# An attention and expert kernel: engine overlap in the scheduler's cost model, and one more head pair transposed by DMA

## The chip, the cores and the metric

The kernel runs on one NeuronCore of a Trainium2 chip. The metric is the device time of one execution in microseconds (us); a kernel's figure is the median of its runs. The clock of TensorE that the hardware granted is known for every run, and no run of this study was in a slow state, so all runs are compared with each other. Engines are named as in the profile: PE is TensorE, PEld its weight load, DVE is VectorE, ACT ScalarE, POOL GpSimd, SP SyncE. GpSimd and SyncE issue DMAs, each into a queue of its own (the rows POOLq and SPq of the page).

## The reference

```python
def _attn_ref(q, k, v):                      # 4 batches x 8 heads x 768 x 64
    k_sum = k.reshape(B, H, nb, 32, D).max(axis=3)      # a summary of each 32 keys
    v_sum = v.reshape(B, H, nb, 32, D).mean(axis=3)
    scores_l = scale * q @ k^T, kept where |pos_q - pos_k| < 16
    scores_s = scale * q @ k_sum^T + log(32)
    a = softmax over both together
    return a @ concat(v, v_sum)

def _moe_ref(x, w_gate, w1, w2):             # x: 3072 x 512, 8 experts, 1024 hidden
    P = exp(x @ w_gate - max)
    8 times: normalize P by rows, by columns, times N / E
    out = sum over e of P[:, e] * (relu(x @ w1[e]) @ w2[e])
```
(Abridged to pseudocode; the attention's output, reshaped, is x.)

## The kernel before

The 32 heads are handled as 16 pairs, two heads of 64 columns side by side. The experts' matmuls are woven between the steps of attention, so that TensorE always has something to do. The weaving is made while the program is built: every step is a unit with an engine, a cost in us, and the units it depends on, and a list scheduler picks the order in which each engine issues its units.

```python
class Plan:
    HOP = 0.15
    ...                                            # (cut)
    def order(self):
        ...
                for e, cost in u.eng.items():      # a unit may have a choice of engines
                    t = max([t0, free.get(e, 0.0)]
                            + [d.end + d.lag + (self.HOP if d.on != e else 0.0) for d in u.deps])
                    best.setdefault(e, []).append((t, u, cost))
        ...
            u.start, u.end, u.on = t, end, e
            free[e] = end                          # the engine is free when its unit ends
```

What comes out is a fixed order for each engine. In these traces an engine that comes to an instruction which must wait stands there (TensorE for 4.28 us in the kernel after). `lag` is the planned time between the end of issuing a DMA and its landing.

The parts of attention that matter here, for a "whole" pair i (4 to 15, made by `pair_whole`; the constant `WHOLE` is another matter). The keys and queries arrive as rows and must be transposed; before pair `BY_DMA` TensorE does it, from there on a DMA transpose from SyncE. The values of one 128-row chunk need 16 rows from each neighbouring chunk; four small copies, SBUF to SBUF by DMA, put them into `V_e`. I call them the **bordering copies**.

```python
    BY_DMA = 12
    X_BY_DMA = 12
    WHOLE = 10
    ...
    def tr(i, z): ...            # 6 TensorE transposes into PSUM, copied out by ScalarE or VectorE
    def tr_dma(i, z):
        st = at.pop(("st", i, z))
        dst = (kT[i % NB][:], qT[i % NB][:, W:W + S])[z]
        nc.sync.dma_start_transpose(out=dst.rearrange("c (g t) -> c g t", g=G),
                                    in_=st[:].rearrange("p g j d -> p (g j d)"))
    ...
    def near_values(i):
        sv, ve = v_x[i % NQ], V_e[i % NE]
        eng = nc.sync if i < BY_DMA else nc.gpsimd
        for j in range(2):
            c0, q0 = VD * j, 64 + 32 * j
            eng.dma_start(out=ve[q0 + W:q0 + 2 * W, 1:G, c0:c0 + VD], in_=sv[128 - W:128, j, 0:G - 1, :])
            eng.dma_start(out=ve[q0:q0 + W, 0:G - 1, c0:c0 + VD], in_=sv[0:W, j, 1:G, :])
    ...
    def values(i, h):            # unit A: exp(scores) times values
        ...                      # 6 matmuls  av <- vx, em   (the chunk itself)
        ...                      # 3 matmuls  av <- Ve, Ee   (borders and summaries: needs V_e)
    ...
        # in pair_start
            if i >= BY_DMA:
                for z in range(2):
                    U["tr", i, z] = add("SP", 1.4, lambda z=z: tr_dma(i, z), ...)
                    U["kT", i, z] = add("DMA", 1.7, None, [U["tr", i, z]], prio, lag=2.0)
    ...
        # in pair_whole
            U["near", i] = add("SP" if i < BY_DMA else "POOL", 2.4 if i < BY_DMA else 3.0,
                               lambda: near_values(i),
                               [U["v", i], U.get(("A", i - NE, 1)), U["vc", i % NE]], prio,
                               lag=5.0 if i < BY_DMA else 3.5)
    ...
            for h in range(2):
                U["A", i, h] = add("PE", 0.4, lambda h=h: values(i, h),
                                   [U["mk", i, h], U["ed", i], U["sx", i, h], U["Vs", i], U["near", i]], ...)
```

So `BY_DMA` sets two things: who transposes a pair's k and q, and whose queue carries its bordering copies. The loads of k, q and v for these pairs are issued from GpSimd. Line numbers of the kernel after are one higher than those of the kernel before (L441 there is L442 here).

Of the kernel before, what the change touches and what calls it, by code (L numbers as in the profile page):

```python
# [33 lines left out]
class Plan:  # L34

    HOP = 0.15

    def __init__(self, slots, idle=None):
        self.units, self.slots = [], slots
# [18 lines left out]
    def order(self):  # L58
        free, ring, turn = {}, {t: [None] * n for t, n in self.slots.items()}, {t: 0 for t in self.slots}
        left, n_left, after = [], {}, {}  # L60
        for u in self.units:
            n_left[u] = len(set(u.deps))
            for d in set(u.deps):
                after.setdefault(d, []).append(u)
            if not u.deps:
                left.append(u)
        done = []

        def ready(u):
            t = 0.0  # L70
            for i, b in enumerate(u.opens):
                old = ring[b.tag][(turn[b.tag] + i) % self.slots[b.tag]]
                if old is not None:
                    if any(x.start is None for x in old.users):
                        return None
                    t = max([t] + [x.end + (self.HOP if x.on not in u.eng else 0.0) for x in old.users])
            return t

        while left:
            best = {}  # L80
            for u in left:
                t0 = ready(u)
                if t0 is None:
                    continue
                for e, cost in u.eng.items():
# [3 lines that stand above are left out]
            picks = []  # L89
            for e, c in best.items():  # L90
                t_min = min(t for t, _, _ in c)
                t, u, cost = min((x for x in c if x[0] <= t_min + 0.02), key=lambda x: x[1].prio)
                picks.append((t, t + cost, e, u, cost))
            t, end, e, u, cost = min(picks, key=lambda x: x[:2])
            if self.idle is not None:
                us, fn, until = self.idle
                if until.start is not None:
                    self.idle = None
                while self.idle is not None and t > free.get("PE", t) + us:
                    x = Unit("PE", us, fn, [], 0.0, [Buffer("m")], 0.0)  # L100
                    x.opens[0].users.append(x)
                    t0 = ready(x)
                    if t0 is None or t0 + us > t:
                        break
                    x.start = max(t0, free["PE"])
                    x.end = free["PE"] = x.start + us
                    if x.end > t:
                        break
                    x.on = "PE"
                    ring["m"][turn["m"] % self.slots["m"]] = x.opens[0]  # L110
                    turn["m"] += 1
                    done.append(x)
            u.start, u.end, u.on = t, end, e
            free[e] = end
            for b in u.opens:
                ring[b.tag][turn[b.tag] % self.slots[b.tag]] = b
                turn[b.tag] += 1
            left.remove(u)
            done.append(u)
            for x in after.get(u, ()):  # L120
                n_left[x] -= 1
                if not n_left[x]:
                    left.append(x)
        assert len([u for u in self.units if u.start is None]) == 0
        return done
# [3 lines left out]
def kernel(  # L129
# [12 lines left out]
    B, H, S, D = q.shape  # L142
# [14 lines left out]
    HG = G // 2  # L157
    VD = D + 1
    NEH = 3
    BY_DMA = 12  # L160
    X_BY_DMA = 12
    WHOLE = 10
    FILL = {"v0": 1, "S0": 1, "s0": 2, "s1": 1, "s2": 1}

    const = ctx.enter_context(tc.tile_pool(name="const", bufs=1))
# [60 lines left out]
    with tc.manual_schedule():  # L226
# [155 lines left out]
        def scores(i):  # L382
            sg = at["sg", i, 0] = banks2("sg")
            dst = [[sg[:, j, :] for j in range(2)], None]
            if i >= WHOLE:
                dst[1] = at["sg", i, 1] = [bank("a", "sg1") for _ in range(2)]
            score_mms(i, dst, range(G if i >= WHOLE else HG))

        def scores_1(i):
            sg = at["sg", i, 1] = banks2("sg")  # L390
# [553 lines left out]
        def pair_whole(i, prio):  # L944
            U["near", i] = add("SP" if i < BY_DMA else "POOL", 2.4 if i < BY_DMA else 3.0, lambda: near_values(i),
                               [U["v", i], U.get(("A", i - NE, 1)), U["vc", i % NE]], prio, lag=5.0 if i < BY_DMA else 3.5)
            x1 = []
            deps = [U["kT", i, 0], U["kT", i, 1], U.get(("ed", i - 2))]
            bufs = [Buffer("s")] + (2 * [None] if i < WHOLE else [Buffer("a"), Buffer("a")])
            U["S", i, 0] = U["S", i, 1] = add("PE", 0.4 if i < WHOLE else 0.6, lambda: scores(i), deps, prio,  # L950
                                              opens=[x for x in bufs if x is not None])
            U["X", i, 0] = add("ACT", 0.97, lambda: score_exp(i, 0), [U["S", i, 0]], prio, uses=bufs[:1])
            if i < WHOLE:
                buf = Buffer("s")
                U["S", i, 1] = add("PE", 0.4, lambda: scores_1(i), deps, prio, opens=[buf])
                U["X", i, 1] = add("ACT", 0.97, lambda: score_exp(i, 1), [U["S", i, 1], U["X", i, 0]], prio,
                                   uses=[buf])
            else:
                x1 = [add("ACT", 0.53, lambda j=j: score_exp(i, 1, j), [U["S", i, 0], U["X", i, 0]], prio,
                          uses=bufs[1 + j:2 + j]) for j in range(2)]  # L960
                U["X", i, 1] = x1[1]
            for h in range(2):
                U["mk", i, h] = add("DVE", 0.56, lambda h=h: masks(i, h),
                                    [U["X", i, h], *x1[:h], U.get(("A", i - 2, 1))], prio)
            U["ed", i] = add("DVE", 0.78, lambda: edges(i),
                             [U["X", i, 0], U["X", i, 1], U["mk", i, 1], U.get(("A", i - NE, 1)), U["ec", i % NE]], prio)
            buf = Buffer("a")
            U["ss", i, 0] = U["ss", i, 1] = add("PE", 0.22, lambda: summaries_2(i),
                                                [U["km", i], U["kT", i, 1], U.get(("A", i - NE, 1))], prio, opens=[buf])
            for h in range(2):  # L970
                U["sx", i, h] = add("ACT", 0.46, lambda h=h: summary_exp(i, h), [U["ss", i, h]], prio, uses=[buf])
            for h in range(2):
                buf = Buffer("a")
                U["A", i, h] = add("PE", 0.4, lambda h=h: values(i, h),
                                   [U["mk", i, h], U["ed", i], U["sx", i, h], U["Vs", i], U["near", i]],
                                   prio, opens=[buf])
                U["no", i, h] = add("DVE", 0.75, lambda h=h: normalize(i, h),
                                    [U["A", i, h], U.get(("x", i - 2))], prio, uses=[buf])
            if i >= X_BY_DMA and i % PB < PB - 1:
                U["xt", i] = add("SP", 1.5, lambda: x_dma(i), [U["no", i, 0], U["no", i, 1]], prio)  # L980
                U["x", i] = add("DMA", 1.7, None, [U["xt", i]], prio, lag=2.0)
                return
            buf = Buffer("a")
            U["xt", i] = add("PE", 0.35, lambda: to_xT(i), [U["no", i, 0], U["no", i, 1]], prio, opens=[buf])
            U["x", i] = add({"ACT": 0.8, "DVE": 0.55}, 0, lambda: x_out(U["x", i].on, i), [U["xt", i]], prio,
                            uses=[buf])
# [109 lines left out]
        def transposed():  # L1096
# [1 line left out]
            r = (NP - 1) % NB  # L1098
            nc.gpsimd.tensor_copy(out=warm[:, 0:1], in_=kT[r][0:32, 0:1])
            nc.gpsimd.tensor_copy(out=warm[:, 1:2], in_=qT[r][0:32, W:W + 1])  # L1100
            if X_BY_DMA < NP:
                nc.gpsimd.tensor_copy(out=warm[:, 4:5], in_=xT[0:32, PB - 2, (B - 1) * S:(B - 1) * S + 1])
            ve = V_e[(NP - 1) % NE]
            for j in range(2):
# [1 line left out]
                                      in_=ve[64 + 32 * j:96 + 32 * j, G - 2, VD * j:VD * j + 1])  # L1106

        last[0] = add("POOL", 0.3, transposed, [last[0], U["near", NP - 1]] + [U["kT", NP - 1, z] for z in range(2)]
                      + [U["x", i] for i in range(X_BY_DMA, NP - 1)])
        load("w1n", lambda: load_w1(1), 0.85, 5.0)  # L1110
        load("w2n", lambda: load_w2(1), 0.85, 5.0)
        U["w1", 1], U["w2", 1] = U["w1n"], U["w2n"]
        U["post"] = add("SP", 0.0, pools, [U["lo", b] for b in range(B)] + [last[0]])
        prev = [U["post"]]
        for n in range(8):
            rows = add("DVE", 1.65, sink_rows, prev, 0)
            buf = Buffer("Q")
            cols = add("PE", 0.1, sink_cols, [rows], 0, opens=[buf], lag=0.1)
            prev = [add("DVE", 0.6, sink_apply, [cols], 0, uses=[buf])]
# [201 lines left out]
```

## Time and profile before

| | before |
|---|---|
| time, median of the first 3 runs | 666.17 us (666.14 to 666.85) |
| span of the profiled run, granted clock | 664.1 us, 0.999 |
| TensorE busy | 99% |
| VectorE, ScalarE, GpSimd busy | 83%, 62%, 30% |
| DMA queue of SyncE (hardware) | 9.58 MB, 5.9% of 16 engines' span |
| pair 11's bordering copies: issued, last landed | 75.81 to 77.72 us from SyncE, 84.70 us |
| pair 11's first border matmul | 92.64 us |

The prediction shows the lines on which the bound rests. What it did not look at are the last two rows of the table: when pair 11's copies land and when TensorE wants them. Times of issue come from the timelines of SyncE and TensorE, times of landing, here and below, from the updates of the DMAs' semaphores in the packed trace; a pair is told apart by counting the groups of four copies and the groups of border matmuls. In the kernel before there are 7.9 us between the two.

### The profile page before, as it was taken

The numbers are of one execution on the slowest core, as the hardware profiler recorded it, in microseconds if no ns is written. First come the engines' busy times: TensorE is split into PE (matmuls) and PEld (weight loads), VectorE is DVE, ScalarE is ACT, GpSimd is POOL, SyncE is SP. The second block draws the span as 40 slices with busy tenths as digits, with TensorE's granted clock in tenths as the row PEclk, the third lists the DMA queues.
The fourth block names the chain that finished last, engine by engine and source line by source line (L and its number), as shares of the span: only waits on it lengthen the run. The fifth ranks groups of instructions, "written<-read, shape, count | busy, mean of one in ns | idle before, by whom it ended". The sixth has DMA issues, their size and how long they took to land.

```text
span 664.1 us, 13257 instructions
## 1 busy us (share of the span) xinstructions
PE 656.6 (99%) x5131; PEld 435.9 (66%) x5132; DVE 550.1 (83%) x1036; ACT 410.9 (62%) x769; POOL 199.0 (30%) x257
## 2 busy tenths in 40 slices
PE   8999999999999999999999999999999999999997
PEld 4666666545766666666666666666666666666666
DVE  7899897799988887887779877988778877988776
ACT  6677676556885566556665665555655656556652
POOL 8899522100132222212322222223122213222123
PEclk9999999999999999999999999999999999999999
DMA  9999932700953747373754665373838465335656
GB/s 167 181 145 145 143 70 43 128 1 2 157 96 65 126 75 118 64 128 65 110 97 71 121 91 101 64 127 65 127 64 135 73 96 96 64 64 112 157 134 202
DMA packets 112558, 67.89 MB, mean 102 GB/s; under 512 B 77936, under 2 KB 90480, under 8 KB 112496
## 3 DMA queue, kind: packets, MB, share of 16 engines
q0 software_dynamic: 94816, 57.46, 64.9%
q1 hardware_dynamic: 17152, 9.58, 5.9%
q8 instruction: 40, 0.66, 0.4%
q14 instruction: 22, 0.18, 0.1%
q10 hardware_dynamic: 528, 0.02, 0.0%
HBM read 52.45 MB, written 6.29 MB: 88 GB/s over the span
## 4 chain that ended last, share of the span: by engine, by line
PE 96%; DVE 3%; DMA 1%; issue 0%; ACT 0%; POOLq 0%; DVEq 0%
PE yps L815 22%; PE pA L764 22%; PE pY L815 17%; PE pQ L764 11%; PE hps L211 6%; PE yps L216 6%; PE pR L764 5%; PE sg L347 1%; DMA qst<-in_q_dram 1%; PE av L512 1%; PE vs L357 1%; PE tkq L303 1%; PE av L435 1%; DVE xs L543 1%; PE ss L461 1%; PE av L441 1%
## 5 line engine op out<-in xcount | busy, mean ns | idle before, releaser
L815 PEld LDWEIGHTS <-h 128*128 128x128 f16 x2352 | 230.1, 98 | 88.5 <-issue 1.0
L843 POOL DMA_DIRECT2D out_acc<-y x120 | 101.7, 891 | 372.1 <-ACT y L839 110.3
L839 ACT ACTIVATE y<-pY,P_sb 128x256 f32<-128x256 f32 x168 | 79.8, 477 | 123.3 <-PE pY L815 121.6
L830 DVE SCALAR_TENSOR_TENSOR out_acc<-yps,P_sb,out_acc 128x512 f32<-128x512 f32 x128 | 95.1, 744 | 29.0 <-PE yps L815 29.0
L798 DVE TENSOR_TENSOR h<-h 128x1024 f16<-128x1024 f16 x168 | 109.3, 683 | 1.4
L815 PE MATMUL pY<-w,h 128*128 128x256 f16 x672 | 100.0, 273 | 0.6 <-ACT y L839 0.6
L815 PE MATMUL yps<-w2sum,h 128*128 128x256 f16 x672 | 98.4, 273 | 0.0
L764 PE MATMUL pA<-xT,w 128*128 128x512 f16 x336 | 98.3, 379 | 0.0
L815 PE MATMUL yps<-w,h 128*128 128x256 f16 x672 | 93.3, 273 | 0.0
L830 DVE SCALAR_TENSOR_TENSOR out_acc<-pY,P_sb,out_acc 128x512 f32<-128x512 f32 x84 | 62.8, 748 | 29.1 <-PE pY L815 27.4
L764 PEld LDWEIGHTS <-w 128*128 128x128 f16 x672 | 65.8, 98 | 31.6 <-issue 0.2
L764 PEld LDWEIGHTS <-w1sum 128*128 128x128 f16 x504 | 49.3, 98 | 45.0
L786 DVE CUSTOM_DVE_ANT_0 h<-pQ,snap 128x512 f16<-128x512 f32 x84 | 57.6, 685 | 7.0 <-ACT snap L207 4.3
L786 DVE CUSTOM_DVE_ANT_0 h<-pA,snap 128x512 f16<-128x512 f32 x84 | 57.3, 682 | 4.8 <-PE pA L764 4.8
L202 ACT ACTIVATE h<-pA 128x512 f16<-128x512 f32 x84 | 50.6, 603 | 12.6 <-PE pA L764 12.4
L202 ACT ACTIVATE h<-pR 128x512 f16<-128x512 f32 x84 | 50.1, 596 | 8.0 <-PE pR L764 7.7
L207 ACT COPY pR<-pA 128x512 f32<-128x512 f32 x83 | 47.5, 572 | 7.7 <-PE pA L764 6.9
L815 PE MATMUL pY<-w2sum,h 128*128 128x256 f16 x336 | 50.4, 273 | 0.0
L764 PE MATMUL pA<-xsum,w 128*128 128x512 f16 x168 | 50.0, 379 | 0.0
L764 PE MATMUL pR<-xT,w 128*128 128x512 f16 x168 | 50.0, 379 | 0.0
L764 PE MATMUL pQ<-xsum,w1sum 128*128 128x512 f16 x168 | 50.0, 379 | 0.0
L764 PE MATMUL pA<-xsum,w1sum 128*128 128x512 f16 x168 | 50.0, 379 | 0.0
(150 smaller groups left out, 854.3 us busy)
## 6 DMA issues: line engine op xcount, KB each, us to landing
out_acc<-y POOLq DMA_DIRECT2D x120, 256.0 KB, 3.4
w<-in_moe_w_dram POOLq DMA_DIRECT2D x14, 1024.0 KB, 10.7
out_dram<-out_acc SPq DMA_DIRECT2D x24, 256.0 KB, 2.4
qst<-in_q_dram POOLq DMA_DIRECT2D x32, 96.0 KB, 5.3
vx<-in_v_dram POOLq DMA_DIRECT2D x15, 192.0 KB, 6.2
kst<-in_k_dram POOLq DMA_DIRECT2D x24, 96.0 KB, 5.6
w<-in_moe_w_dram POOLq DMA_DIRECT2D x4, 256.0 KB, 7.6
w<-in_moe_w_dram POOLq DMA_DIRECT2D x2, 512.0 KB, 7.7
```

What stands on the lines that cost most here:

```text
L202: nc.scalar.activation(out=out, in_=in_, func=AF.Relu, bias=0.0, scale=1.0)
L207: (nc.scalar.copy if eng == "ACT" else nc.vector.tensor_copy)(out=out, in_=in_)
L211: nc.tensor.matmul(hp[:, 0:n], lhsT=w1s[e][:, dk, f * 128:(f + 1) * 128], rhs=xT[:, dk, t0:t0 + n], start=(dk == 0), stop=(dk == KD - 1))
L216: nc.tensor.matmul(yp[:, d], lhsT=h[:, f, c * 128:(c + 1) * 128], rhs=w2s[e][:, f, d], start=(f == 0), stop=(f == KF - 1))
L303: nc.tensor.transpose(t[:, g * 128:(g + 1) * 128], st[:, g, :, :].rearrange("p j d -> p (j d)"), ident)
L764: nc.tensor.matmul(dst[:], lhsT=lhsT, rhs=rhs, start=first and k == 0, stop=k == HK - 1, skip_group_check=True)
L786: nc.vector._custom_dve(dve_ops.TENSOR_ADD_SAT, out=ring(e, p, q)[:, q % 2, blk, :], in0=at[src, e, p, q][:], in1=at.pop(("snap", n, e, p, ...
L798: nc.vector.tensor_tensor(out=h[:, :, out_, :], in0=h[:, :, a, :], in1=h[:, :, b, :], op=op)
L815: nc.tensor.matmul(dst[:, d], lhsT=lhsT, rhs=rhs, start=f == 0 and n in (1, 5, 2), stop=f == HF - 1, skip_group_check=True)
L830: nc.vector.scalar_tensor_tensor(out=o, in0=y, scalar=scalar, in1=o, op0=ALU.mult, op1=ALU.add)
L839: nc.scalar.activation(out=at[key][:, d], in_=src, func=AF.Copy, bias=0.0, scale=P_sb[:, t, e:e + 1])
L843: nc.gpsimd.dma_start(out=o, in_=at.pop(("y", e, p, c, key))[:], accum_op=ALU.add)
```

## The change

Two intents. The scheduler takes an engine as busy to the end of each unit, though VectorE and ScalarE start the next instruction a little before the last one has ended (0.08 and 0.09 us before, by the medians in the prediction); the change gives back 0.07 and 0.09 us for each unit and corrects one figure (sink rows, 1.65 to 1.5 us). And one more pair is transposed by DMA, which takes 12 transposes off TensorE.

```diff
+    OVERLAP = {"DVE": 0.07, "ACT": 0.09}
...
-            free[e] = end
+            free[e] = end - self.OVERLAP.get(e, 0.0)
...
-    BY_DMA = 12
-    X_BY_DMA = 12
-    WHOLE = 10
+    BY_DMA = 11
+    X_BY_DMA = {12, 13, 14}
+    WHOLE = {10, 11, 12, 13, 14, 15}
...
-            rows = add("DVE", 1.65, sink_rows, prev, 0)
+            rows = add("DVE", 1.5, sink_rows, prev, 0)
```

(Cut: the places that test `i in WHOLE` and `i in X_BY_DMA` in place of `>=`; the sets hold the same pairs as before.) What the diff doesn't say in words: with `BY_DMA = 11`, pair 11's bordering copies go from SyncE's queue to GpSimd's.

The text on record follows, with marks where passages are cut: statements of how the hardware behaves that no trace of this case shows. No term of its sum is cut: that is 0.67 us for the transposes and 0.22 us for fewer breaks between kinds, together 0.89 us, off 666.17, which gives 665.3 us. Its estimate of the time that the columns of all matmuls need is cut. The trace of the kernel before gives one in its place: the medians of 56 ns for 128 columns and 216 ns for 512 make 0.417 ns a column, and at that, each column counted once, an estimated 638.3 of the 664.1 us are columns. Three statements that stay, with their figures from the same trace: a matmul of 256 columns has a bar of 273 ns in the median and the next starts 109 ns after it; none of SyncE's 69 DMAs lands before an earlier one of SyncE; the DMA share between 40 and 80 us is 2.29.

> **What bounds the kernel now.** I read the page first: the table of busy time, the forty slices, then the chain that ended last.
>
> ```profile
> span 664.1 us, 13257 instructions
> ...
> PE 656.6 (99%) x5131; PEld 435.9 (66%) x5132; DVE 550.1 (83%) x1036; ACT 410.9 (62%) x769; POOL 199.0 (30%) x257
> ...
> PE   8999999999999999999999999999999999999997
> ...
> PEclk9999999999999999999999999999999999999999
> ...
> PE 96%; DVE 3%; DMA 1%; issue 0%; ACT 0%; POOLq 0%; DVEq 0%
> ```
>
> TensorE is busy in every slice but the first and the last, at the full clock, and 96% of the chain that ended last is TensorE work. VectorE, the next, has 17% of the span free. A change that only moves work between VectorE and ScalarE can therefore gain only where TensorE really waits for one of them.
>
> "Busy" is not enough to say so, because each matmul's bar overlaps the next one's. So I took the start of every matmul in the trace and the distance to the next start. Matmuls of 512 columns start 216 ns apart in the median, those of 256 columns 109 ns, those of 128 columns 56 ns. From 24 us on, three places alone show a wait beyond what a change from one group of matmuls to the next normally costs: 0.21 us before the logits at 65.9 us, 0.30 us (0.17 + 0.12) between 644.6 and 645.4 us, and 0.73 us at 657.5 us. In all 1.24 us in 640. The last of them is visible in the timeline of the tail:
>
> ```profile
> 657.21 0.60 PE L815 MATMUL pY<-w2sum,h 128*128 128x256 f16 x4
> 657.85 0.47 ACT L839 ACTIVATE y<-pY,P_sb 128x256 f32<-128x256 f32 x1 [2.09 <-PE pY L815]
> 658.37 0.60 PE L815 MATMUL pY<-w,h 128*128 128x256 f16 x4 [0.56 <-ACT y L839]
> ```
>
> A group adds into the bank that ScalarE is still reading; TensorE cannot go round it.
>
> [...]
>
> [...]VectorE's h sums last 682 ns in the median, yet the next instruction starts a median 602 ns after the start; ScalarE's copies into pR last 570 ns with 483 ns to the next start. It is seen in pairs in the timeline too:
>
> ```profile
> 647.52 0.83 ACT L839 ACTIVATE y<-pY,P_sb 128x256 f32<-128x256 f32 x2
> ...
> 651.10 1.46 DVE L830 SCALAR_TENSOR_TENSOR out_acc<-yps,P_sb,out_acc 128x512 f32<-128x512 f32 x2
> ```
>
> Two y of 0.47 us each fit in 0.83 us. So the new constants, 0.07 us for VectorE and 0.09 us for ScalarE, bring the scheduler's picture nearer the chip. Nothing runs faster for it: the constants only change the order in which instructions are issued, and which of two engines takes a copy.
>
> **The change part by part.**
>
> 1. Overlap and the sink figure (1.65 to 1.5 us). No instruction is added or removed. The built programs agree on TensorE in their first 655 rows (327 matmuls, up to 24.3 us in the trace of before) and in the last 49; between them the order differs. Copies shift to VectorE: snapshots from pA 29 to 40, from pQ 14 to 23, first scalings 6 to 10, while hidden relus go 17 to 10 the other way. That is 24 more and 7 fewer of these four kinds on VectorE. At some 0.6 us (from start to start) about 10 us of work moves to an engine with 114 us free. Cost on the path: none of itself.
>
> 2. Pair 11's q and k by DMA. This removes 12 TensorE transposes, 6 for k and 6 for q:
>
> ```profile
> 80.69 0.51 PE L303 MATMUL tkq<-ident,kst 128*128 128x128 bf16 x6
> 81.03 1.03 PE L216 MATMUL yps<-w,h 128*128 128x512 f16 x4
> ...
> 82.55 0.50 PE L303 MATMUL tkq<-ident,qst 128*128 128x128 bf16 x6
> 82.88 1.46 PE L211 MATMUL hps<-xT,w 128*128 128x384 f16 x8
> ```
>
> Measured from start to next start, not by the second column: 81.03 - 80.69 = 0.34 us and 82.88 - 82.55 = 0.33 us. Since TensorE has no free time there, **0.67 us** comes off the end. Two VectorE copies of 0.56 us out of PSUM go too, beside the path.
>
> What is added is two DMA transposes on the queue that issues from SyncE. [...]The trace has eight like them, and the row of the values that border on a chunk, which move from SyncE's queue to GpSimd's for this pair:
>
> ```profile
> Ve<-vx SPq DMA_DIRECT2D x32, 10.2 KB, 5.1
> ...
> Ve<-vx POOLq DMA_DIRECT2D x16, 10.2 KB, 1.9
> kT<-kst SPq DMA_TRANSPOSE x4, 5.5
> qT<-qst SPq DMA_TRANSPOSE x4, 4.9
> ```
>
> In before, pair 11's k and q have been requested by 58 us and its scores run at 84.28 us. A transpose issued near 66 us, where pair 12's now stands (66.23 us), would land near 72. The bordering values cost GpSimd four issues of 0.52 us right after its last value load (76.62 us) and should land near 82, about when SyncE's (75.81 us plus four issues and 5.1 us) did. So nothing of this lands on the path.
>
> 3. The new order as TensorE sees it. I priced each matmul of both built programs, from 24.3 us on, with the median start-to-next-start that the same kind with the same successor has in before (7 changes of kind in the new order have no equal there and got their kind's median). The new order comes out 0.89 us shorter: the 0.67 us above, and 0.22 us from fewer breaks between kinds. That is an estimate for an order without waits.
>
> Sum: 0.89 us off 666.17 gives 665.3. Of the 1.24 us of waits some may go, but the one of 0.73 us stands in the 49 last rows that do not change.
>
> **The rivals.** (a) New waits on TensorE. The old, pessimistic constants left slack: instructions came ready earlier than planned. With truer constants TensorE is asked for results closer to when they are there. For it: hundreds of dependent steps between 24 and 160 us. Against it: 0.07 and 0.09 us are still below the 0.08 to 0.09 us that I read. Expert matmuls fill that stage, so a late result holds TensorE for tenths of a us. I allow 0 to 1.5 us; then 665.3 to 666.8. (b) The waits at 65.9 and 645 us vanish and the logits come early, as the order suggests (the last logits stand 28 matmuls earlier, 12 of them the transposes): up to 0.5 us more gained, 664.8. (c) The transposes of pair 11 or the bordering values behind them come late, because SyncE's queue is in order and DMA is loaded to over twice its engines' time between 40 and 80 us. Pair 11 would be late by a few us, and filler would run instead only if the fixed order has it. It would cost 1 to 4 us, 666 to 669. The 12 us computed above speak against it. (d) VectorE becomes the bound among the experts: no, 10 us more of 550 leave it under 86%.
>
> **Range and chances.** Centre 665.3 us, from the sum with (a) and (b) about cancelling. Low 664.3: the sum with (b) and half a us of run-to-run spread (the three runs of before span 0.7 us). High 666.5: most of (a), no net gain. Two per cent is 13.3 us; ten times the removed waits would not make it, and only a broken order would cost it. Faster 0.01, same 0.98, slower 0.01.
>
> **What would show it right or wrong.** Right: 84 transposes into tkq from the later pairs instead of 96, TensorE's busy time about 0.7 to 0.9 us lower, its slices all 9 from the second to the last but one, the wait of about 0.7 us for y still there at the end, pair 11's kT landing 5 to 6 us after issue with no TensorE wait before its scores, VectorE some us busier and ScalarE less. Wrong: TensorE idle or stretched starts between 24 and 160 us that sum to over 1 us (rival a or c; the waits name which), or a gain over 1.5 us, which would mean that waits were hidden in the starts that I took as normal changes between groups.

## The result, and the profile after

The kernel after takes **675.4 us** in the median (674.15 to 676.8, 4 runs); the kernel before, with one more run beside them, 666.27 us (666.14 to 666.85, 4 runs). The ratio is **1.0134**, with a 95% interval of 1.0115 to 1.0153. A ratio here is the mean time of one kernel's fast runs over that of the other's in the same rounds, so it is not quite the ratio of the medians. At a threshold of 2% the verdict is still "same", yet the loss of 9 us lies far outside the spread. It is some ten times the predicted gain, with the other sign.

The page of the kernel after, the lines that answer to the prediction's first fence:

```profile
span 673.5 us, 13253 instructions
...
PE 661.0 (98%) x5119; PEld 436.9 (65%) x5120; DVE 563.0 (84%) x1051; ACT 401.6 (60%) x752; POOL 201.5 (30%) x261
...
PE   9999979999999999999999999999999999999997
...
PEclk9999979999999999999999999999999999999999
...
PE 92%; DMA 6%; POOL 1%; issue 0%; ACT 0%; DVE 0%; SPq 0%; POOLq 0%; ACTq 0%; DVEq 0%
```

TensorE has 12 matmuls fewer, VectorE 13 us more and ScalarE 9 us less, all as meant. But one slice, the sixth (84 to 101 us), has lost both TensorE work and clock, and DMA has gone from 1% to 6% of the chain that ended last. The table by stretches of time narrows it down. Its columns are the stretch, its length, busy us (and instructions) of PE, PEld, DVE, ACT and POOL, the granted clock, the DMA share and GB/s. First the kernel before, then the kernel after:

```profile
80.00:100.00 20.00, 20.00 (x206) 12.47 (x205) 17.73 (x47) 15.78 (x28) 4.27 (x8) 1.00 0.68 79
```

```profile
60.00:80.00 20.00, 20.00 (x233) 13.23 (x231) 14.36 (x40) 16.75 (x30) 17.04 (x21) 1.00 2.28 137
80.00:100.00 20.00, 14.54 (x117) 9.03 (x116) 12.09 (x32) 8.14 (x15) 5.24 (x10) 0.83 1.08 104
100.00:120.00 20.00, 20.00 (x215) 12.10 (x215) 14.19 (x41) 15.37 (x30) 4.46 (x10) 1.00 0.20 35
```

Between 80 and 100 us the kernel before ran 206 matmuls, the kernel after 117. The stretches beside it are full. To weigh this, I took at a given time the time less the columns of all matmuls before the one under way, at the 0.417 ns a column of the two medians (56 ns for 128 columns, 216 ns for 512): an estimate of what TensorE is behind a row of columns without a break. Before, it is 9.31 us at 80 us and 9.02 at 100 us; after, 9.89 and 18.78. The difference between the kernels grows from 0.58 to 9.76 us in this stretch, and hardly more in the remaining 570 us. So **the whole loss arises between 80 and 100 us**. The timeline of TensorE there, kernel after (start, us, engine, line, operation, tile written <- tiles read, form, count, and in brackets the idle time before it with what ended it):

```profile
81.67 0.36 PE L436 MATMUL av<-vx,em 128*128 128x65 bf16 x6
83.37 0.52 PE L442 MATMUL av<-Ve,Ee 128*128 128x130 bf16 x3 [1.33 <-DVE Ee L421]
...
87.45 1.46 PE L212 MATMUL hps<-xT,w 128*128 128x384 f16 x8
88.75 0.35 PE L436 MATMUL av<-vx,em 128*128 128x65 bf16 x6
93.22 0.50 PE L442 MATMUL av<-Ve,Ee 128*128 128x130 bf16 x3 [4.12 <-DMA Ve<-vx]
...
94.81 1.49 PE L212 MATMUL hps<-xT,w 128*128 128x384 f16 x4
```

And pair 11's values in the kernel before, the same two groups:

```profile
92.45 0.35 PE L435 MATMUL av<-vx,em 128*128 128x65 bf16 x6
92.64 0.34 PE L441 MATMUL av<-Ve,Ee 128*128 128x130 bf16 x3
```

The losses are, with waits from start to start:

1. **4.28 us** from the last `vx,em` matmul of pair 11 (88.91 us) to its first `Ve,Ee` (93.22 us), less the usual 0.03 us. The releaser is a bordering copy. The kernel before has no wait at this place, and comes to it 3.7 us later in the run.
2. **1.50 us** before pair 10's `Ve,Ee` at 83.37 us, released by VectorE's border scores (`Ee`).
3. **A half-speed clock.** Four hps matmuls (the experts' first product) take 1.49 us at 94.81, eight take 1.46 us at 87.45. The trace grants half the clock (0.50) from 91.88 to 98.71 us, 6.83 us; TensorE works in 5.5 us of it (93.22 to 98.71), which costs an estimated 2.7 us, half of that. In this trace the granted clock is 1.00 through the wait of 1.50 us and falls to 0.50 during that of 4.28 us; whether the wait is the cause, f_fill below tries. If it is, the wait is here paid for about 1.6 times (4.28 + 2.7 over 4.28).

Together 1.50 + 4.28 + 2.7 = 8.5 us of the 9.2; the rest is small changes between groups that I did not take apart.

Why did the copies land so late? GpSimd's timeline, kernel after:

```profile
76.81 1.03 POOL L290 DMA_DIRECT2D vx<-in_v_dram  x1
77.83 0.57 POOL L378 DMA_DIRECT2D Ve<-vx  x1
78.48 0.55 POOL L380 DMA_DIRECT2D Ve<-vx  x1
83.03 0.53 POOL L378 DMA_DIRECT2D Ve<-vx  x1 [4.00 <-DMA vx<-in_v_dram]
85.05 0.53 POOL L380 DMA_DIRECT2D Ve<-vx  x1 [1.50 <-DMA kst<-in_k_dram]
```

The four copies stand right behind the last loads, those of pair 15. GpSimd issued two, then stood 4.00 us until an earlier load had landed, issued one, and stood 1.50 us for another. In the traces of the kernel before and the kernel after no engine has more than eight DMAs of its own under way (GpSimd 8 and 8, SyncE 7 and 8), and the packed trace of the kernel after tells why GpSimd stands: its DMAs here use eight semaphores in turn, and these two issues carry a wait for the very semaphore that they use. They start 0.28 us after the DMA eight before had landed (at 82.75 and 84.77 us). So these waits are the program's own. The chain of waits tells the rest:

```profile
73.03 12.03 DMA kst<-in_k_dram
85.05 8.03 DMA Ve<-vx
93.08 0.14 issue
93.22 0.50 PE av L442 x3
```

The landing of a load of k let GpSimd issue the last copy, and that took another 8.03 us. (The view names the load issued at 73.03 us, but that one landed at 86.38; by the semaphores it was its neighbour, issued at 71.82 and landed at 84.77 us.) The copy issued first, at 77.83 us, landed at 91.93, 14.1 us later, directly behind pair 15's value load (issued 76.81, landed 91.71). A copy of 10.2 KB sat out what its queue already held: in the traces of the kernel before and the kernel after none of the 464 DMAs issued from GpSimd (230 and 234), and none of the 136 from SyncE (69 and 67), lands before an earlier one of the same engine. The range for all copies from 55 to 100 us, first the kernel before, then the kernel after:

```profile
DMA to landing us min/median/max: 1.7/4.9/7.1
```

```profile
DMA to landing us min/median/max: 1.7/5.8/14.1
```

The plan knows nothing of this: for copies from GpSimd it has 3.0 us of issuing and 3.5 us to landing (`U["near", i]` above), whatever else is in the queue. Here it was 7.8 and 7.5 us.

The loads themselves had become slower: those of pair 15 took 12.3 to 14.9 us from issue to landing, in the kernel before 7.5 to 9.0 us. The timeline of SyncE shows what else was on the way. Kernel before:

```profile
75.81 0.58 SPq L377 DMA_DIRECT2D Ve<-vx  x1
...
77.72 0.59 SPq L379 DMA_DIRECT2D Ve<-vx  x1
78.48 2.25 SPq L330 DMA_TRANSPOSE kT<-kst  x1
```

Kernel after:

```profile
70.78 1.22 SPq L331 DMA_TRANSPOSE kT<-kst  x1
...
73.59 3.58 SPq L331 DMA_TRANSPOSE kT<-kst  x1
77.34 2.78 SPq L331 DMA_TRANSPOSE qT<-qst  x1
```

In the kernel before, pair 11's copies also held up the queue: pair 13's transposes stood behind them until 78.48 us, and most of those of the last two pairs ran when the loads were done or nearly so. With the copies gone, the transposes of pairs 11, 12 and 13 all fall among the loads. Issues to landing of kT<-kst went from a median of 5.5 us to:

```profile
kT<-kst SPq DMA_TRANSPOSE x5, 8.5
qT<-qst SPq DMA_TRANSPOSE x5, 9.1
```

A transpose of k, 192 KB (two loads of 96 KB fill its source), landed as early as 2.71 us after issue in the kernel before, when the loads were over (issued at 85.87 us); the five of the kernel after took 6.62 to 10.62 us.

The earlier wait, that of 1.50 us, comes from the late transposes too. VectorE, kernel after:

```profile
79.94 0.95 DVE L336 TENSOR_REDUCE ks<-kT 128x24 bf16<-128x768 bf16 x1 [3.87 <-DMA kT<-kst]
...
82.70 0.19 DVE L421 TENSOR_TENSOR Ee<-er,band 32x80 bf16<-32x80 bf16 x1
```

VectorE stood 3.87 us before the key maximum of pair 12, whose transpose took 9.1 us (70.78 to 79.92). The border scores of pair 10 are behind it in VectorE's order, and TensorE waited for them.

That is a reading. The experiments ask which part of it carries the 9 us.

### The profile page after: what moved, and what is told of

Same layout as the page of the kernel before. It is cut to its first block, busy times and chain, and to the rows that moved or that the text cites. A ratio compares the mean times of both kernels' runs of the same rounds, so it can differ in the third digit from the quotient of the medians.

```text
span 673.5 us, 13253 instructions
## 1 busy us (share of the span) xinstructions
PE 661.0 (98%) x5119; PEld 436.9 (65%) x5120; DVE 563.0 (84%) x1051; ACT 401.6 (60%) x752; POOL 201.5 (30%) x261
## 4 chain that ended last, share of the span: by engine, by line
PE 92%; DMA 6%; POOL 1%; issue 0%; ACT 0%; DVE 0%; SPq 0%; POOLq 0%; ACTq 0%; DVEq 0%
PE yps L816 22%; PE pA L765 22%; PE pY L816 16%; PE pQ L765 11%; PE pR L765 5%; PE hps L212 5%; PE yps L217 5%; DMA kst<-in_k_dram 2%; DMA Ve<-vx 2%; DMA vx<-in_v_dram 1%; DMA qst<-in_q_dram 1%; PE sg L348 1%; PE av L513 1%; PE vs L358 1%; PE av L442 1%; PE tkq L304 1%
## 5 line engine op out<-in xcount | busy, mean ns | idle before, releaser
L816 PE MATMUL yps<-w2sum,h 128*128 128x256 f16 x672 | 100.3, 273 | 0.0
L816 PE MATMUL yps<-w,h 128*128 128x256 f16 x672 | 90.3, 273 | 0.0
L212 PE MATMUL hps<-xT,w 128*128 128x384 f16 x256 | 50.8, 332 | 0.0
L765 PE MATMUL pQ<-xT,w1sum 128*128 128x512 f16 x168 | 50.0, 379 | 0.2 <-ACT snap L208 0.2
```

The source lines that it names most:

```text
L212: nc.tensor.matmul(hp[:, 0:n], lhsT=w1s[e][:, dk, f * 128:(f + 1) * 128], rhs=xT[:, dk, t0:t0 + n], start=(dk == 0), stop=(dk == KD - 1))
L765: nc.tensor.matmul(dst[:], lhsT=lhsT, rhs=rhs, start=first and k == 0, stop=k == HK - 1, skip_group_check=True)
L816: nc.tensor.matmul(dst[:, d], lhsT=lhsT, rhs=rhs, start=f == 0 and n in (1, 5, 2), stop=f == HF - 1, skip_group_check=True)
```

## The experiments

My theory, Q: pair 11's bordering copies come late because they are now at the end of GpSimd's queue behind loads. Rivals: V, the new order of VectorE and ScalarE (the overlap constants) makes the late results; T, the two more transposes by themselves slow everything. "The kernel before" is measured anew in each batch (666.15 to 666.21 us). All kernels gave correct results, and all runs were fast.

### Undoing one thing: the queue of pair 11's copies

```diff
 # after -> a_near11_sp (order of TensorE, VectorE and ScalarE unchanged)
-            eng = nc.sync if i < BY_DMA else nc.gpsimd
+            eng = nc.sync if i < BY_DMA + 1 else nc.gpsimd
```

> The changed kernel, but pair 11's four bordering-value copies go through SyncE's queue again (one line; TensorE, VectorE and ScalarE keep the changed kernel's order exactly). Theory Q (queue): the loss of 9 us comes from these copies standing behind the last pairs' loads in GpSimd's queue, and from pair 13 and 14's transposes no longer being held back behind them. Then the copies land 6 to 8 us after issue, by 85 us, values of pair 11 do not wait, the clock stays full: 665 to 667 us. Rival T (transposes): pair 11's two extra DMA transposes crowd the DMA engines and all transfers land late; then 669 us or more and TensorE still waits for a landing between 80 and 95 us.

Measured: 668.51 us (668.35 to 669.68), ratio 1.0037 (1.0022 to 1.0052), the clock full (means of 0.999 to 1.0). The copies landed at 83.97 us; pair 11's values no longer wait:

```profile
87.62 0.51 PE L551 MATMUL tx<-ident_x,xs 128*128 128x128 f16 x6 [2.17 <-DVE xs L544]
...
89.27 0.35 PE L436 MATMUL av<-vx,em 128*128 128x65 bf16 x6
89.45 0.34 PE L442 MATMUL av<-Ve,Ee 128*128 128x130 bf16 x3
```

Nothing but the issuing engine of four DMAs differs (which also puts pair 13's transposes behind them again), and 6.9 us of the 9 are back. That speaks for Q. The remaining 2.3 us are in the first line: TensorE waits for VectorE, which waited 2.46 us for a transposed k of pair 13 (issued 76.87, landed 85.43). My expected figure missed this; the late transposes stay.

### One part alone: only BY_DMA = 11

```diff
 # before -> b_bydma11
-    BY_DMA = 12
+    BY_DMA = 11
```

> The kernel before with only the second part of the change: pair 11's q and k by DMA transpose and its bordering values through GpSimd, old scheduling constants. By the stall-free price of its order, the values of pair 11 start near 91 us instead of 86 us. Theory Q: the copies land near 92 to 93 us here too, but little waits for them: 666 to 669 us, with a wait of 1 to 2 us for them. Rival O (only the overlap constants hurt): 665.5 us, no wait. Rival T: 672 us or more.

Measured: 672.16 us (671.18 to 673.35), ratio 1.0083 (1.0066 to 1.01). The same wait, without any overlap constant:

```profile
91.45 0.35 PE L435 MATMUL av<-vx,em 128*128 128x65 bf16 x6
95.98 0.50 PE L441 MATMUL av<-Ve,Ee 128*128 128x130 bf16 x3 [4.18 <-DMA Ve<-vx]
```

It is 4.35 us from start to start, followed by half the clock for 6.83 us. Rival V isn't needed for the wait. By my own mark, 672 us or more, this result is rival T's, and the transposes do take part: the same queue without them (d_near11_pool, below) loses nothing. I had expected 1 to 2 us, reckoning with copies that land as in the kernel after: here they were issued later as well (82.43 to 87.77 us) and landed at 95.85.

### One part alone: only the overlap and the sink figure

```diff
 # after -> c_overlap
-    BY_DMA = 11
+    BY_DMA = 12
```

> The kernel before with only the first part of the change: overlap constants and the sink figure, pair 11 transposed on TensorE and its bordering values through SyncE. Theory Q: no loss, 665.5 to 667 us; values of pair 11 start near 87 us and their copies land by then. Rival O (truer constants leave no slack and TensorE waits for VectorE and ScalarE): 669 us or more, with waits between 24 and 160 us that are not for a DMA.

Measured: 668.17 us (666.81 to 669.19), ratio 1.0027 (1.0008 to 1.0045). The runs fall into two groups, 666.81 and 667.24, 669.11 and 669.19. So the new constants alone gain nothing; they cost about 1.8 us, where theory Q had expected no loss. The profiled run is of the faster group. A wait that its trace shows is at pair 6, far ahead of what I was looking at, for copies from SyncE's own queue:

```profile
51.86 0.40 PE L442 MATMUL av<-Ve,Ee 128*128 128x130 bf16 x3 [0.44 <-DMA Ve<-vx]
```

### The other half: pair 11's copies on GpSimd, all else as before

```diff
 # before -> d_near11_pool
-            eng = nc.sync if i < BY_DMA else nc.gpsimd
+            eng = nc.sync if i < BY_DMA - 1 else nc.gpsimd
```

> The kernel before with only one thing moved: pair 11's four bordering-value copies go through GpSimd's queue instead of SyncE's; TensorE's order is unchanged and its values of pair 11 start near 92.3 us. Theory Q: the copies land with or just after pair 15's v, several us later than the 84.7 us of before, and pairs 13's transposes are issued about 5 us sooner; but values of pair 11 come so late that the time stays at 666 to 668 us. If the copies land before 86 us, the queue is not what made them late.

Measured: 666.59 us (666.14 to 667.89), ratio 1.0008 (0.9993 to 1.0023). The copies were issued from 77.24 to 81.91 us, landed at 87.89 us at the latest, 3.2 us later than in the kernel before, and were hidden, because in the old order TensorE comes to them at 92.8 us. The queue alone is harmless, if nothing else is late and nothing asks earlier.

### The same with the new order

```diff
 # c_overlap -> i_ov_near11_pool
+    NEAR_SP = 11                      # pairs below this: copies from SyncE
-            eng = nc.sync if i < BY_DMA else nc.gpsimd
+            eng = nc.sync if i < NEAR_SP else nc.gpsimd
 # and likewise in the unit U["near", i]
```

> The overlap-only kernel (668.17 us), but pair 11's bordering-value copies go through GpSimd's queue behind all loads; pair 11 is still transposed on TensorE, and TensorE, VectorE and ScalarE keep the overlap-only kernel's order. Its values of pair 11 start near 87 us. If the queue place is enough in this earlier order, the copies land at 88 to 91 us and TensorE waits 1 to 4 us: 669 to 674 us. If it takes the extra transposes as well, no wait for them: 667 to 669 us.

Measured: 668.45 us (667.79 to 671.65), ratio 1.0042 (1.0017 to 1.0066). Now TensorE comes to pair 11's copies at 88.59 us, they land at 90.07, and it waits 1.59 us. With c_overlap (copies from SyncE, landed 82.11) there was none at this place. The wait is in the range that I expected, the median is not. The profiled runs differ by 1.5 us (668.74 and 667.24), the medians by 0.3, as the runs of c_overlap fall into two groups. All the cases together, in us of the profiled runs:

| kernel | order | k, q of pair 11 by | copies from | last issued | last landed | TensorE ready | wait | median |
|---|---|---|---|---|---|---|---|---|
| before | old | TensorE | SyncE | 77.72 | 84.70 | 92.61 | none | 666.2 |
| d_near11_pool | old | TensorE | GpSimd | 81.91 | 87.89 | 92.79 | none | 666.59 |
| b_bydma11 | old constants | DMA | GpSimd | 87.77 | 95.85 | 91.61 | 4.35 | 672.16 |
| c_overlap | new | TensorE | SyncE | 75.04 | 82.11 | 88.75 | none | 668.17 |
| i_ov_near11_pool | new | TensorE | GpSimd | 81.77 | 90.07 | 88.59 | 1.59 | 668.45 |
| a_near11_sp | new | DMA | SyncE | 76.12 | 83.97 | 89.42 | none | 668.51 |
| after | new | DMA | GpSimd | 85.05 | 93.08 | 88.91 | 4.28 | 675.4 |

Read by columns: GpSimd's queue makes the copies land 3 to 8 us later, the transposes by DMA push their last issue and landing out by another 3 to 8 us, and the new order asks 3 to 4 us sooner. The kernel before had 7.9 us to spare, and the three together need more. T by itself is not the cause: a_near11_sp has all the transposes and no wait for copies. Nor is the new order needed: b_bydma11 has the queue and the transposes alone, and its wait of 4.35 us is as long as that of the kernel after. The 3.2 us between these two kernels are about what the wait of 1.50 us and the cost of c_overlap come to; I did not take them apart further.

### The place in the queue, nothing else

```diff
 # after -> h_near_first (same engine, same queue; orders of TensorE, VectorE, ScalarE unchanged)
 # in load_pair, the loads of k and q:
-                         1.2 if i < PB else 1.4, [U.get(("tr", old, z)), U.get(("tr", old, 2))], ...)
+                         1.2 if i < PB else 1.4,
+                         [U.get(("tr", old, z)), U.get(("tr", old, 2)), U["near", 11] if i == 15 else None], ...)
```

> The changed kernel, but the loads of pair 15 are put behind pair 11's bordering-value copies in GpSimd's queue; same queue, and TensorE, VectorE and ScalarE keep the changed kernel's order exactly. Theory Q (place in the queue): the copies land before 86 us, no wait of 4 us for them, full clock: 667 to 670 us, about as with SyncE's queue (668.5 us). Rival: GpSimd's queue itself, or the DMA engines' load, makes them late wherever they stand: 673 us or more.

Measured: 668.1 us (666.8 to 668.69), ratio 1.0025 (1.0008 to 1.0042).

```profile
87.67 0.35 PE L436 MATMUL av<-vx,em 128*128 128x65 bf16 x6
88.64 0.40 PE L442 MATMUL av<-Ve,Ee 128*128 128x130 bf16 x3 [0.62 <-DMA Ve<-vx]
```

The copies stay on GpSimd but go ahead of pair 15's loads of k, q and v. They are issued from 75.56 us, land by 88.50, and the wait falls from 4.28 to 0.79 us. The time is as expected, the landing is not (I had said before 86 us): the copies land right behind pair 14's value load (issued 74.35, landed 87.55 us), which still stands in front of them. So most of the loss is not GpSimd as such; it is what stands in front.

### What the clock costs: filling the wait

```diff
 # after -> f_fill, in values(i, h), ahead of the first matmul into av (zeros times zeros, overwritten by it)
+            if (i, h) == (11, 0):
+                for _ in range(10):
+                    stream(av, 512)
```

> The changed kernel, with ten matmuls of zeros of 512 columns (2.15 us at full clock) put ahead of pair 11's first values, into the same bank, overwritten after; VectorE's, ScalarE's and the DMA queues' orders are unchanged. In the changed kernel TensorE stands idle for 4.28 us there and its clock is then granted at half for 6.83 us, in which 2.9 us are lost. If the idle stretch is what lowers the clock, it shrinks to about 2.1 us, the clock stays full and the time falls to about 672.5 us, although work was added and the copies land no sooner. If the lower clock has another cause, the time stays at 675 us or rises.

Measured: 673.82 us (672.53 to 674.3), ratio 1.011 (1.0094 to 1.0125).

```profile
88.69 2.32 PE L617 MATMUL av<-zeros 128*128 128x512 bf16 x9
90.85 0.35 PE L439 MATMUL av<-vx,em 128*128 128x65 bf16 x6
94.10 0.40 PE L445 MATMUL av<-Ve,Ee 128*128 128x130 bf16 x3 [2.90 <-DMA Ve<-vx]
95.02 0.81 PE L212 MATMUL hps<-xT,w 128*128 128x384 f16 x4
```

The first line shows nine of the ten fillers in one group; the tenth has no record, but the first two starts are 0.43 us apart, twice the usual distance. The span and mean granted clock of this run:

```profile
core 0: 671.7 us, clock 1.000
```

In this run the idle time is 3.07 us, and the clock stays full (1.000): four hps matmuls take 0.81 us in place of 1.49. The kernel is 1.6 us *faster* with 2.15 us of useless work more (2.16 us by the timeline, 88.69 to 90.85). The account closes: work and wait together are 5.22 us in place of 4.28 (the copies landed 0.9 us later this time), less the 2.7 us of half clock, gives −1.8 us. So in the profiled run the clock's share of the loss is shown, not only argued. The filler does not always save it: of the four runs two had the full clock (673.46 and 672.53 us) and two a mean of 0.996 and 0.997 (674.3 and 674.18 us), and the latter are the slower ones.

### Telling the scheduler the truth about the transposes

If late DMAs are the matter, the plan should know of it. The plan has a transpose land 5.1 us after the start of its issue (1.4 to issue, 1.7 and lag 2.0); the trace of the kernel after says 8.5. With lag 6.0 the plan has 9.1.

```diff
 # after -> g1_lag6
+    NEAR_SP = 12                      # pair 11's copies planned and issued on SyncE
-            eng = nc.sync if i < BY_DMA else nc.gpsimd
+            eng = nc.sync if i < NEAR_SP else nc.gpsimd     # and in U["near", i]
-                    U["kT", i, z] = add("DMA", 1.7, None, [U["tr", i, z]], prio, lag=2.0)
+                    U["kT", i, z] = add("DMA", 1.7, None, [U["tr", i, z]], prio, lag=6.0)
```

> A try at a better version: the changed kernel with pair 11's copies planned on SyncE again and the scheduler told that a transposed k or q lands 6.0 us after the transfer's turn instead of 2.0 us (the traces show 5 to 10 us from issue), so that VectorE is not ordered to take the key maximum before it can. Theory: the 2.3 us wait for xs that remained with SyncE's queue (VectorE standing before the key maximum of pair 13) goes: 665 to 667 us. If late transposes hold VectorE elsewhere, 668 us again.

Measured: 665.62 us (665.51 to 665.98), ratio 0.999 (0.9976 to 1.0005). The big waits are gone. This looked like the predicted 665.3, so I ran the same kernel again on another chip with five rounds:

> The same kernel as the try with 6.0 us of landing time and pair 11's copies on SyncE, timed in five rounds to settle a difference under one per cent. Expected again 0.4 to 0.9 us under the kernel before (665.6 against 666.2 us), the 0.89 us of the stall-free price less some tenths lost near 50 to 56 us. If it is only luck of one chip: ratio 1.000 or above.

Measured: 666.66 us (665.65 to 667.34), ratio 1.0003 (0.999 to 1.0017). No gain that holds. What differs is seen at pair 6, first in g1_lag6, then in g1_again:

```profile
51.04 0.35 PE L437 MATMUL av<-vx,em 128*128 128x65 bf16 x6
51.22 0.34 PE L443 MATMUL av<-Ve,Ee 128*128 128x130 bf16 x3
```

```profile
51.04 0.35 PE L437 MATMUL av<-vx,em 128*128 128x65 bf16 x6
52.49 0.40 PE L443 MATMUL av<-Ve,Ee 128*128 128x130 bf16 x3 [1.10 <-DMA Ve<-vx]
```

The same program, and TensorE at the same point at the same time; pair 6's copies landed at 49.77 us in one run and at 52.35 in the other, and TensorE wants them at 51.2. This is the slack that the old constants had left.

### The truth about the transposes, copies left on GpSimd

```diff
 # after -> l_lag6_pool
-                    U["kT", i, z] = add("DMA", 1.7, None, [U["tr", i, z]], prio, lag=2.0)
+                    U["kT", i, z] = add("DMA", 1.7, None, [U["tr", i, z]], prio, lag=6.0)
```

> The changed kernel with the 6.0 us landing time alone; pair 11's copies stay in GpSimd's queue. Two separate waits in the changed kernel: 1.5 us for the edges (VectorE held by a late kT) and 4.28 us for the copies, with 2.9 us of half clock after. If they are separate, the first goes and the second stays: 672 to 675 us. If late transposes were behind both, 668 us or less.

Measured: 676.49 us (674.49 to 677.52), ratio 1.0148 (1.0129 to 1.0167), though the 1.50 us wait of the kernel after is gone.

```profile
87.78 0.35 PE L436 MATMUL av<-vx,em 128*128 128x65 bf16 x6
95.49 0.51 PE L442 MATMUL av<-Ve,Ee 128*128 128x130 bf16 x3 [7.36 <-DMA Ve<-vx]
```

TensorE comes 1 us sooner to a landing that is later (95.44 us) and waits 7.53 us, then has half the clock for 10.24 us. My expected figure missed here. Removing the earlier wait gained nothing, because the end of the longer one is set by the DMA queue: TensorE only comes to it sooner. As the landing moved too, the run does not show what the 1.50 us are worth with the landing in place; by the same reckoning they could not be won back alone.

### Is the rest of the change worth something?

```diff
 # g1_lag6 -> k_no_overlap
-    OVERLAP = {"DVE": 0.07, "ACT": 0.09}
+    OVERLAP = {}
 # and sink_rows 1.5 -> 1.65
```

> The better version without the overlap constants and with the old sink figure: pair 11 by DMA, its copies on SyncE, 6.0 us of landing time. If the gain is the 12 transposes removed and the waits avoided, 665.3 to 666 us, as good as with the overlap constants: then these give nothing of themselves. If they matter to the gain: 666.5 us or more.

Measured: 668.26 us (668.12 to 670.76), ratio 1.0037 (1.002 to 1.0054), the second of the two outcomes that I had named. Its waits are elsewhere, 0.76 us at 124.8 us and some 2.2 us between 164 and 180 us. Beside g1_again (666.66 us in the same batch) the overlap constants with the sink figure do help, so they are not bad in themselves.

```diff
 # c_overlap -> g2_overlap_lag6: lag=2.0 -> lag=6.0 for the transposes, BY_DMA = 12
```

> The overlap-only kernel (668.17 us) with the 6.0 us landing time; pair 11 transposed on TensorE, its copies on SyncE. If the 2 us that the overlap constants cost alone come from VectorE being ordered to wait for late transposes, they go: 666 to 666.8 us. If they come from elsewhere (the 0.6 us for edges at 51 us, before any DMA transpose), 667 us or more.

Measured: 666.22 us (666.16, 666.18, 666.26 and one of 670.24), ratio 1.0013 (0.9988 to 1.0037). Even with the kernel before, as expected if late transposes are behind it: with the longer landing time the 1.8 us of c_overlap are gone in three of four runs.

With the main cause shown, it stayed open whether a version of the change gains its 0.9 us once the copies from SyncE are planned as late as they come. Two runs gave them more lag on top of g1_lag6:

```diff
 # g1_lag6 -> m_lag85, m_lag75, in U["near", i]
-                               ..., lag=5.0 if i < NEAR_SP else 3.5)
+                               ..., lag=8.5 if i < NEAR_SP else 3.5)      # m_lag75: 7.5
```

> The better version with one more landing time corrected: the bordering-value copies from SyncE are taken to land 8.5 us after their last issue instead of 5.0 us (the traces show 5 to 8 us). Its stall-free price is 0.16 us under that of the version before it, and it orders the values of pair 6 at 56.2 us instead of 50.9 us. If the 0.6 to 1.3 us that were lost near 51 us in two runs are a wait for these copies without slack, the loss goes in every run: 665.2 to 665.8 us, ratio under 1.000 with its interval. If TensorE is held elsewhere by the truer constants: 666.3 us or more.

> The same with 7.5 us instead of 8.5 us. Values of pair 6 at 54.3 us; priced like the better version. Expected 665.3 to 666 us; slower than the kernel before only if pair 11's values, ordered at 86.5 us, or some other step meet a late DMA again.

Measured: 666.66 us (665.82 to 667.93), ratio 1.0009 (0.9995 to 1.0022), and 667.77 us (667.71 to 669.24), ratio 1.0029 (1.0016 to 1.0041). Both missed what I expected. The wait for pair 6 is gone in m_lag85, but others come, of 0.38 us at 57.95 and 0.26 us at 67.64. m_lag75 has six of 0.2 to 0.5 us; the list of waits shows the commonest kind, three waits on VectorE (us in all, how many, the longest):

```profile
PE ss L463 <- DVE ksT L343: 0.8, 3, 0.3
```

No version beat the kernel before by a gain that came again.

**What stays open.** Why c_overlap falls into two groups of runs is shown only in part (pair 6's copies land earlier or later); what makes them do so I did not find. In g1_again SyncE issued the last two 1.9 us later than in g1_lag6; in c_overlap they went out in time and the last took 7.1 us. That transposes and loads slow one another is read from landing times that grew together; no run measures one without the other. The waits at eight DMAs under way are in the program; whether the chip has a limit of its own is not known. No run gave the plan a truer figure for copies from GpSimd. The wait for the copies was never simply left out, since TensorE would then read them too early; it was moved, shortened or filled.

## Why the prediction was wrong, by its steps

- **What bounds the kernel**: right. TensorE bounds the kernel before and after, and the 9 us are TensorE's time. (Its estimate of the time in columns is cut; by the slope of the trace it is the 638.3 us given beside it.)
- **The transposes, 0.67 us off TensorE**: right as to the instructions. Of the pairs by TensorE there are 84 transposes (42 + 42). Whether 0.67 us came off the end no run shows, as no version gained.
- **Pair 11's transposes land in time**: right for TensorE, which doesn't wait for them; they landed at 70.64 and 74.17 us, where the prediction had 72. The time from issue to landing over all pairs was off: 8.5 and 9.1 us in the median, where the prediction had 5.5 and 4.9. Through VectorE, the late transposes of the *next* pair then cost the wait of 1.50 us, which the prediction had not thought of.
- **"The bordering values cost GpSimd four issues of 0.52 us right after its last value load (76.62 us) and should land near 82 ... So nothing of this lands on the path."** This is the step that failed. They landed at 93.08 us. The prediction took 1.9 us to landing from a row of 16 copies in the kernel before. Of those, pair 12's, the first, were issued from 87.93 us on, when the loads were over (the last had landed at 84.48 us), so the figure is that of copies with no load in front. Behind loads the kernel after shows 8.0 to 14.1 us, and issuing itself stretched from about 2 to 7.8 us (77.83 to the end at 85.58), as GpSimd had to wait for landings between the copies. The other half of the same sentence failed unspoken: it asked when the copies come, not when they are wanted. The new order wants them at 88.9 us in place of 92.6; a landing at 93.08 would have been 0.5 us late for the kernel before. Mending the landing is enough (a_near11_sp, and nearly so h_near_first), and in the old order d_near11_pool hides a landing 3.2 us later than before. But the earlier demand is not needed for a loss: b_bydma11, which asks at 91.6 us, waits 4.35 us for a landing at 95.85.
- **The order estimate, 0.89 us less**: not seen. g1_lag6 came to 665.62 us once, and its repeat at 666.66 doesn't confirm it.
- **Rival (a), waits from lost slack, 0 to 1.5 us**: right in kind and nearly in size. c_overlap, which is the overlap without anything else of weight, costs some 1.8 us by its ratio, and pair 6's copies show one way: 0.60 us of wait in its profiled run, and with g1_lag6's program 1.27 us in one run and none in another. One reading speaks against the rival wrongly: ScalarE's new constant of 0.09 us is not below what was read (570 less 483 ns are 0.087 us). The prediction had let it cancel with (b), of which little came: the wait near 645 us went from 0.30 to 0.18 us. The 0.73 us before y at the end is still there, as predicted.
- **Rival (c), bordering values late, 1 to 4 us**: the right mechanism, waved off with "The 12 us computed above speak against it". Those 12 us were for the transposes' landing, not for the copies. Its size was too small too, since half the clock came with this wait (an estimated 2.7 us, which f_fill's account bears out). The prediction's own sign of being wrong came with it: waits of over 1 us between 24 and 160 us, which name rival (c).
- **Rival (d), VectorE the bound**: rightly dismissed. VectorE is at 84%.
- **Range and chances**: 664.3 to 666.5 us did not hold the 675.4. The spread was built from the rivals (a) and (b) alone; (c) was left out of it. The chances named "within 2%", and that held, but only because 2% are 13.3 us.

## What to carry to other kernels

When a small transfer moves to another queue, look up what that queue holds at that moment, and take the time to landing from transfers issued behind a like load (8.0 to 14.1 us here), not from a median of copies that had none in front (1.9 us). Then compare two times, when it lands and when the *new* order wants it, and ask what the old queue had been holding back. In a planned order, a truer cost for the engines removes slack that was covering DMA landings which the plan has too short; correct both together or neither. And look at the granted clock after a long TensorE wait: the three here of 4.28, 4.35 and 7.53 us cost an estimated 1.4 to 1.6 times their length, with half of the time that TensorE worked at half clock added, while in the profiled run of f_fill the clock was full after one of 3.07 us. More than these four cases the runs do not show.
